# Turning the gathered tokens of experts 2 to 7 by a transposing DMA in place of TensorE transposes

## The chip, the cores and the metric

The kernel runs on one core of one Trainium2 chip. A core has five engines that run on their own and meet by semaphores: TensorE (PE: matrix products from SBUF into PSUM; PEld is its loading of weights), VectorE (DVE), ScalarE (ACT), GpSimd (POOL) and SyncE (SP). Each works through its own queue of instructions in order. DMAs are issued by SP, ACT or POOL. The metric is the device time of one execution in microseconds (us), less is better.

## The reference

Eight batches of pooled attention feed a mixture of eight experts. Every token goes to one expert, and every expert takes `cap` = 4608 / 8 = 576 tokens. Cut to what matters here:

```
x = attention(q, k, v)                 # [4608, 512]
logits = x @ w_gate
# tokens are assigned greedily by falling logit, 576 to an expert
for e in range(8):
    mask = assigned == e
    h = np.maximum(x[mask] @ w1[e], 0.0)   # w1[e]: [512, 1024]
    out[mask] = h @ w2[e]                  # w2[e]: [1024, 512]
```

## The kernel before

Attention comes first (to about 153 us) and writes x to DRAM as `xd`. The experts then run one after the other, in an order that the routing finds while the experts before them run. "Expert 3" below is the fourth in that order.

**Gather.** For one expert `X.gather` (L1035) brings 576 rows of 512 float32 numbers from `xd` into `xg` [128, 5, 512], with one indirect DMA of POOL for each of five token tiles: four of 128 tokens and one of 64. Here a partition holds a token.

**Turn.** A product needs the feature, not the token, along the partitions. So `X.xt(t)` (L1064) turns tile t: four transposes of TensorE (L1073) put it into a PSUM buffer `tp`, ACT copies that to `xh` rounded to the format of fast products (L1075), and DVE puts the rest, what rounding has left over, into `xl` (L1077). `xh` and `xl` [128, 4, 576] have one buffer each.

**Weights.** w1 and w2 of an expert come by SP (L1024, L1032; 2 MB each) into one raw buffer each and are cut in the same way into a high part by ACT (`w1h` L1049, `w2h` L1059) and a low part by DVE (`w1l` L1053, `w2l` L1062), eight pieces each. The load of the next w2 waits until the products of the last token tile (L1136), which read raw w2, are done.

**First stage** (`stage1`, L1079). h = x w1 in two column blocks: tokens 0 to 255 (tiles 0 and 1), then 256 to 575 (tiles 2 to 4), eight groups each. A group is twelve products (L1097) into one of five PSUM buffers `h`; ACT evicts it to `hh` (L1102, in the second block also `hr`, L1104), DVE the rest to `hl` (L1105).

**Second stage** (`stage2`, L1117). For each of four token tiles 24 products (L1131), then ACT copies `yt` out (L1145) and POOL scatters it to the output; the last tile of 64 tokens has 32 products of raw float32 (L1136).

**The order.** Nothing reorders at run time. The function `experts` (L1206) writes all queues out ahead with a planner: `now` counts PE's time as products are issued, `dve` when DVE will be free, and `advance` puts the steps of the routing in where their inputs should be ready. The routing of the next expert is a search on DVE with small products of PE between (`cmp` on DVE L631, then `rt` products L676; `g` on DVE, then `rt` L697; `up` on DVE, and again), four rounds of it, then the numbers of the rows (L785, L804) and the gather. `turns` places a turn once the gather should have landed; tiles 0 to 2 of the next expert go into the second stage of the expert before, tiles 3 and 4 into its own first stage, mostly right behind an `rt` product. The gather of an expert is held back until all five tiles of the expert before are turned.

Of the kernel before, what the change touches and what calls it, by code (L numbers as in the profile page):

```python
# [11 lines left out]
BF = mybir.dt.bfloat16  # L12
F16 = mybir.dt.float16
I32 = mybir.dt.int32
AF = mybir.ActivationFunctionType
OP = mybir.AluOpType
AX = mybir.AxisListType
# [406 lines left out]
class Routing:  # L424
# [28 lines left out]
    def consts(self, jp, ident):  # L453

        nc, cst, J, NC = self.nc, self.cst, self.J, self.NC
        self.ident = ident
        t = self.ti
        self.i36 = cst.tile([128, 36], F32, name="i36")
        nc.vector.tensor_copy(self.i36, t)
        self.tokv = cst.tile([128, NC], F16, name="tokv")  # L460
        nc.vector.tensor_copy(self.tokv, self.tok.rearrange("p b q -> p (b q)"))
        self.j16 = cst.tile([128, J, NC], F16, name="j16")
        nc.scalar.activation(self.j16, self.i36[:, :J, None].to_broadcast([128, J, NC]), AF.Copy)
# [151 lines left out]
    def search(self, shadow, spare):  # L615
# [8 lines left out]
        def compare(*cuts):  # L624
            qb = q16.rearrange("p (b c) -> p b c", c=4)
            for b0, b1 in zip(cuts, cuts[1:]):
                nc.vector.tensor_tensor(cmp[:, b0:b1], qb[:, b0:b1, None].to_broadcast([128, b1 - b0, J, 4]),
                                        self.j16[:, None, :, :4].to_broadcast([128, b1 - b0, J, 4]), op=OP.is_gt)

        def pairs():  # L630
            nc.vector.tensor_tensor(cmp.rearrange("p b j c -> p (b j c)").rearrange("p (c j u) -> p c j u", j=J // 2, u=2),  # L631
# [89 lines left out]
    def close(self, k, last):  # L721
# [46 lines left out]
        def number(b0, b1):  # L768
# [4 lines left out]
        number(*halves[0])  # L773
        OHa = wk.tile([128, 9, 32, 4], F16, name="OHa", bufs=1)
        nc.vector.tensor_tensor(OHa, sf[:, 0].rearrange("p (b q) -> p b q", q=4)[:, :, None].to_broadcast([128, 9, 32, 4]),
                                self.j16[:, None, :, :4].to_broadcast([128, 9, 32, 4]), op=OP.is_equal)
        if not k:
            block(*halves[1])
        yield 2.6, 2.6
# [208 lines left out]
class Experts:  # L988
# [1 line left out]

    def __init__(self, tc, wk, psA, xd, w1, w2, out, ident, cap):
        self.tc, self.nc, self.wk, self.psA = tc, tc.nc, wk, psA
        self.xd, self.w1, self.w2, self.out, self.ident = xd, w1, w2, out, ident
# [64 lines left out]

    def low2(self, e, i):
        self.nc.vector.tensor_tensor(self.w2l[:, i], self.raw2[e][:, i], self.w2h[:, i].bitcast(F32), op=OP.subtract)  # L1062

    def xt(self, t, name="tp", bufs=2, later=lambda after, t, f: f()):  # L1064

# [94 lines left out]
@with_exitstack  # L1160
def kernel(ctx, tc, q, k, v, wblk, moe_w1, moe_w2, out):
    nc = tc.nc
    N, Dm = out.shape
    cap = N // moe_w1.shape[0]
    cst = ctx.enter_context(tc.tile_pool(name="cst", bufs=1))
    dr = ctx.enter_context(tc.tile_pool(name="dr", bufs=1, space=DRAM))
    ctx.enter_context(tc.manual_schedule())
    xd = dr.tile([N, Dm], F32, name="xd")
    lg = cst.tile([128, N // 128, 8], F32, name="lg")
    psR = ctx.enter_context(tc.tile_pool(name="psR", bufs=1, space=PSUM))  # L1170
    A = Attention(tc, cst, psR, q, k, v, wblk, xd, lg)
    rwk = ctx.enter_context(tc.tile_pool(name="rwk", bufs=2))
    R = Routing(tc, cst, rwk, psR, lg, cap)
    A.consts()
    R.first()
    NC = N // 128
    with ExitStack() as c2:
        g = R.run()

        R.poke = lambda numbers: wake(nc, rwk, moe_w2, numbers)  # L1180
        bounds = R.bounds(rwk, NC - 12)
        step = lambda: next(bounds, None)
        start = lambda: next(g)
        A.run(c2, R.ones, lambda: R.consts(A.jp, A.ident), R.more, {NC - 11: [step], NC - 10: [step], NC - 9: [step], NC - 8: [lambda: R.best(0, NC - 8)],
                                                       NC - 7: [start], NC - 6: [start, lambda: wake(nc, rwk, moe_w2, R.ti[:32, 0:1])]},
              R.begin(g), R.warm)
    with ExitStack() as c2:
        rows = cst.tile([128, 6], I32, name="lastrows")

        def keep():  # L1190
            nc.vector.tensor_copy(rows[:, :5], R.rows)
            nc.vector.tensor_copy(rows[:, 5:], R.halves)


        X, flag, ps = experts(c2, tc, g, R, xd, moe_w1, moe_w2, out, A.ident, cap, keep)
        fast, X.scatters, X.fixed = X.scatters, [], True
        with tc.If(flag > 0):  # L1197
# [8 lines left out]
def experts(ctx, tc, g, R, xd, w1, w2, out, ident, cap, keep):  # L1206
# [6 lines left out]
    X = Experts(tc, wk, psB, xd, w1, w2, out, ident, cap)  # L1213

    toks, since, pieces, turned = {}, {}, {}, {}
    held, waiting = [], []

    lows = 0

    fresh, coming, through = False, False, False  # L1220

# [13 lines left out]
    def step(e):  # L1235
# [9 lines left out]
        if what == "id":  # L1245

            if p > e or p and pieces[p - 1].l < 8:
                held.append((p, crit, t, what))
                return False
            X.load_1(R.eid, 0, 4 if p else 2)  # L1250
            eids[p] = R.eid
        elif what == "rows":
            if p and turned[p - 1] < 5:
                held.append((p, crit, t, what))
                return False
            X.gather(R.rows, *R.found)
            if R.found[1] == 5:
                toks[p] = R.rows, R.halves
                turned[p] = 0
# [7 lines left out]
    def advance(e, t, quiet=False):  # L1267

        nonlocal now, fresh
        now += t  # L1270
        fresh = False
        while True:
            if waiting and waiting[0][0] <= now:
                flush(len(waiting) - 1)
            elif ready > now or quiet or first(e) or not step(e):
                break

    def due(e, what, t):
        return (e, what) in since and now >= since[e, what] + t
# [44 lines left out]
    def turn(e, t, name="tp", bufs=2):  # L1324
# [9 lines left out]
        elif (e, t) == (0, 4):  # L1334
            later(1.0, 0.2, lambda: X.load_2(behind(1)))

    def turns(e, upto, late):

        nonlocal last
# [33 lines left out]
    for e in range(8):  # L1373
# [5 lines left out]
        for n, dt in enumerate(X.stage1(later, not e)):  # L1379
# [2 lines left out]
                w1.by(4 + (k + 2) // 8)  # L1382
            if not e and 2 <= n < 96:
                turns(e, 5, 5)
            if n == (84 if e else 40):
                for t in range(turned[e], 5):
                    turn(e, t)
            if n >= 64 and n % 2:
                w2.by((n - 70) // 14 if n > 70 else 0)
            if not more and n == 48:  # L1390
# [5 lines left out]
            elif not more and n == 136:  # L1396
                flag = nc.values_load(flag[0:1, 0:1], min_val=0, max_val=1)
            advance(min(e + 1, 7), dt)
            if e and n < 96:
                turns(e, 5, 3 + (n - 14) // 24)  # L1400
        while w2.l < 8:
            w2.next()
        w1 = pieces[e + 1] = Pieces(e + 1, X.high1, X.low1)
        for n, dt in enumerate(X.stage2(e, *toks[e], range(5 if more else 1))):

            advance(min(e + 1, 7), dt, n >= 96)
            if more and due(e + 1, "id", 9):
                w1.by((n - 60) // 12 if n > 60 else 0)
            if more:
                turns(e + 1, 3, (n - 52) // 12)  # L1410
        if more:
            while e + 1 not in toks:
# [1 line left out]
                step(e + 1)  # L1414
            while w1.l < 4:
                w1.next()
            for t in range(turned[e + 1], 2):
                turn(e + 1, t)
        flush(2)
    flush()  # L1420
    ps = psB.tile([128, 512], F32, name="h", bufs=5)
# [85 lines left out]
```

## Time and profile before

| | |
|---|---|
| time, median of 3 runs | 609.72 us (608.83 to 611.48) |
| the profiled execution's own time | 608.98 us |
| its span in the profile | 607.2 us |
| first and second stage of expert 3 | 28.4 and 27.7 us |
| transposes of gathered tokens, L1073 | 160 (20 for an expert) |

The rows of the profile read as follows. A timeline row has start, busy time, engine, line, operation, output<-inputs, partitions x elements, count, and in brackets the idle time before it with what ended it. Times overlap, since products are pipelined: what an instruction costs its engine is read from the start of it to the start of the next. A row of waits has who waited for whom, total us, times, longest. A row of stages has the stretch, its length, then each engine's busy time.

### The profile page before, as it was taken

How to read it: one execution, taken by the hardware profiler on the slowest of the kernel's cores; microseconds unless marked ns; L12 is line 12 of the kernel's file. 1: busy time of each engine (PE TensorE's matmuls, PEld its weight loads, DVE VectorE, ACT ScalarE, POOL GpSimd, SP SyncE). 2: the span in 40 equal slices, each digit the busy share in tenths (PEclk: the TensorE clock that was granted, in tenths of full speed). 3: DMA queues.
4: the chain of work that ended last, by engine and by line, in shares of the span. 5: the costliest groups of instructions: out<-in, count | busy, mean ns of one | idle time of the engine just before them, and what ended most of it. 6: DMA issues, size and time to landing. Idle time of an engine off the chain costs nothing.

```text
span 607.2 us, 11497 instructions
## 1 busy us (share of the span) xinstructions
PE 588.4 (97%) x4316; PEld 518.5 (85%) x4316; DVE 398.9 (66%) x1187; ACT 239.2 (39%) x562; POOL 177.5 (29%) x222
## 2 busy tenths in 40 slices
PE   8999999985999999999999999999999999999996
PEld 5999999983798799879978987898799889888975
DVE  7678878987896789678972885498278338503400
ACT  7444444461461434333532442254236325513411
POOL 2999999101200500522112301130230123011012
PEclk9999999995999999999999999999999999999999
DMA  8999972223531743418103701640181037014011
GB/s 357 416 425 419 403 284 74 81 98 99 157 125 39 231 166 108 143 40 315 46 36 114 286 1 52 221 161 19 53 320 45 35 135 265 2 52 167 1 40 43
DMA packets 32641, 92.23 MB, mean 152 GB/s; under 512 B 3489, under 2 KB 3489, under 8 KB 29889
## 3 DMA queue, kind: packets, MB, share of 16 engines
q1 hardware_dynamic: 21296, 62.92, 27.6%
q0 software_dynamic: 5952, 19.01, 9.2%
q10 hardware_dynamic: 5328, 9.48, 4.2%
q8 instruction: 35, 0.57, 0.4%
q14 instruction: 30, 0.24, 0.1%
HBM read 72.53 MB, written 18.87 MB: 151 GB/s over the span
## 4 chain that ended last, share of the span: by engine, by line
PE 81%; DVE 8%; issue 7%; ACT 1%; DMA 1%; POOL 1%; POOLq 0%; ACTq 0%; another core or an unknown queue 0%; DVEq 0%
PE h L1097 30%; PE h L1131 25%; PE psa L272 7%; PE pss L227 6%; PE h L1136 4%; PE tp L1073 3%; PE pse L256 2%; PE rt L256 1%; PE rt L676 1%; DVE e L238 1%; PE rt L638 1%; DMA out_dram<-yt,rows 1%; PE rt L217 1%; DMA xg<-xd,rows 1%; PE rt L785 1%
## 5 line engine op out<-in xcount | busy, mean ns | idle before, releaser
L1131 PE MATMUL h<-w2h,hh 128*128 128x512 f32 x256 | 101.5, 396 | 0.3 <-PEq L1197 0.3
L1131 PE MATMUL h<-w2l,hh 128*128 128x512 f32 x256 | 101.0, 395 | 0.0
L1131 PE MATMUL h<-w2h,hl 128*128 128x512 f32 x256 | 100.6, 393 | 0.0
L1111 POOL DMA_INDIRECT out_dram<-yt,rows x29 | 29.4, 1013 | 241.0 <-ACT yt L1145 240.3
L1105 DVE SCALAR_TENSOR_TENSOR hl<-h,hh 128x320 fp32r<-128x320 f32 (+1 forms) x128 | 57.0, 452 | 60.7 <-ACT hh L1102 42.6
L1102 ACT ACTIVATE hh<-h 128x320 fp32r<-128x320 f32 (+1 forms) x128 | 52.6, 411 | 107.3 <-PE h L1097 101.7
L1097 PE MATMUL h<-xh,w1h 128*128 128x320 f32 (+1 forms) x512 | 93.2, 300 | 0.2 <-issue 0.2
L1097 PE MATMUL h<-xl,w1h 128*128 128x320 f32 (+1 forms) x512 | 92.3, 299 | 0.0
L1097 PE MATMUL h<-xh,w1l 128*128 128x320 f32 (+1 forms) x512 | 91.2, 297 | 0.0
L1097 PEld LDWEIGHTS h<-xh,w1h 128*128 128x128 f32 x512 | 75.6, 189 | 3.4 <-issue 3.2
L1097 PEld LDWEIGHTS h<-xl,w1h 128*128 128x128 f32 x512 | 75.9, 189 | 0.4
L1097 PEld LDWEIGHTS h<-xh,w1l 128*128 128x128 f32 x512 | 75.8, 189 | 0.0
L1041 POOL DMA_INDIRECT xg<-xd,rows x40 | 40.9, 1023 | 91.4 <-DVE rows L808 53.1
L1145 ACT ACTIVATE yt<-h 128x512 f32<-128x512 f32 x32 | 19.1, 597 | 109.4 <-PE h L1131 77.8
L272 PE MATMUL psa<-vblk,eT 128*128 128x146 f32 (+3 forms) x390 | 59.9, 302 | 0.2
L1131 PEld LDWEIGHTS h<-w2h,hh 128*128 128x128 f32 x256 | 48.1, 188 | 9.5 <-issue 0.7
L1131 PEld LDWEIGHTS h<-w2l,hh 128*128 128x128 f32 x256 | 48.1, 188 | 9.5
L1131 PEld LDWEIGHTS h<-w2h,hl 128*128 128x128 f32 x256 | 48.1, 188 | 9.0
L272 PEld LDWEIGHTS psa<-vblk,eT 128*128 128x128 f32 (+1 forms) x390 | 50.9, 179 | 1.8 <-POOL kblk L176 0.3
L1077 DVE TENSOR_TENSOR xl<-tp,xh 128x512 fp32r<-128x512 f32 (+1 forms) x40 | 25.3, 632 | 36.5 <-ACT xh L1075 35.2
L1053 DVE TENSOR_TENSOR w1l<-raw,w1h 128x512 fp32r<-128x512 f32 x64 | 41.1, 683 | 8.8 <-ACT w1h L1049 8.6
L1062 DVE TENSOR_TENSOR w2l<-raw,w2h 128x512 fp32r<-128x512 f32 x64 | 43.2, 682 | 3.0 <-ACT w2h L1059 2.8
(225 smaller groups left out, 898.0 us busy)
## 6 DMA issues: line engine op xcount, KB each, us to landing
raw<-in_moe_w_dram SPq DMA_DIRECT2D x64, 512.0 KB, 5.3
xd<-xt ACTq DMA_DIRECT2D x36, 256.0 KB, 6.5
rawv<-in_v_dram SPq DMA_DIRECT2D x7, 1280.0 KB, 14.1
rawk<-in_k_dram SPq DMA_DIRECT2D x7, 1152.0 KB, 13.2
rawq<-in_q_dram SPq DMA_DIRECT2D x7, 1152.0 KB, 10.4
rawk<-in_k_dram SPq DMA_DIRECT2D x2, 576.0 KB
rawv<-in_v_dram SPq DMA_DIRECT2D x1, 768.0 KB
rawq<-in_q_dram SPq DMA_DIRECT2D x1, 640.0 KB, 9.0
```

The lines of the kernel that those rows point to most:

```text
L227: nc.tensor.matmul(ps[cols, j // 2, 144 * (j % 2):144 * (j % 2) + 144], self.q_of(b, j, n, cols.stop - cols.start), self.kblk[b % 4][:, j] ...
L272: self.nc.tensor.matmul(o[h], self.eT[i][:, c, h], self.vblk[b % 4][:, self.BLOCKS[c]:self.BLOCKS[c + 1]], start=(c == cs[0]), stop=(c == ...
L1041: nc.gpsimd.indirect_dma_start(out=self.xg[:n, t, :], out_offset=None, in_=self.xd, in_offset=bass.IndirectOffsetOnAxis(ap=rows[:n, t:t + ...
L1053: self.nc.vector.tensor_tensor(l, raw, h.bitcast(F32), op=OP.subtract)
L1062: self.nc.vector.tensor_tensor(self.w2l[:, i], self.raw2[e][:, i], self.w2h[:, i].bitcast(F32), op=OP.subtract)
L1077: later(1.3, 0.65, lambda: nc.vector.tensor_tensor(xl, ps[:, :, :n], xh, op=OP.subtract))
L1097: nc.tensor.matmul(ps[:, :m], a[:, j, fs], b[:, j, o], start=(n == 0), stop=(n == 11))
L1102: nc.scalar.activation(hh[:, f, o], ps[:, :m], AF.Relu)
L1105: later(0.65, 0.4, lambda f=f, o=o, m=m, ps=ps: nc.vector.scalar_tensor_tensor(hl[:, f, o], ps[:, :m], 0.0, hh[:, f, o].bitcast(F32), op0= ...
L1111: st = nc.gpsimd.indirect_dma_start(out=rows, out_offset=bass.IndirectOffsetOnAxis(ap=idx, axis=0), in_=y, in_offset=None)
L1131: nc.tensor.matmul(ps, a[:, f, o], b[:, f], start=(f == 0 and k == 0), stop=(f == 7 and k == 2))
L1136: nc.tensor.matmul(ps[64 * a:64 * a + 64, :256], self.hr[:, f], self.raw2[e][:, f, 256 * a:256 * a + 256], start=(f == 0), stop=(f == 7))
```

## The change

For experts 2 to 7 the five turns by TensorE go, and each tile takes this way instead:

1. `split(t)`: ACT reads the gathered tile as 16-bit numbers and writes two planes, the low halves and the high halves of all 512 features, into `planes` [128, 2, 512]; ACT then issues a DMA that stores them in DRAM (`xs`).
2. `swap(t)`: SP issues a transposing DMA, which reads the 256 rows of 512 16-bit numbers of a tile from `xs` and writes them turned into the place in `xg` from which the tile came. Since low and high halves of a token are neighbouring rows, they end as neighbours, and the result read as float32 is the turned tile.
3. `high(t)`: ACT rounds it into `xh`, from SBUF now; `low(t)`: DVE puts the rest into `xl`.

The planner orders the four steps: `swap` 4.4 us of its clock after the split, `high` 8.6 after it, `low` 0.8 after `high`. Splits are at least 2.3 apart. `hurry` lets a step that writes `xh` or `xl` pass only when the first stage of the expert before is behind it (`xfree`). The splits of experts 3 to 7 may thus begin in the first stage of the expert before, those of expert 2 in the second stage of expert 1. The gather of each of the experts 3 to 7 is held until `low` has run for all five tiles of the expert before. `j16`, a table of constants, shrinks from 36 columns to 4. Experts 0 and 1 keep their TensorE turns.

```diff
+    def split(self, t):
+        nc = self.nc
+        n = min(128, self.cap - 128 * t)
+        p = self.wk.tile([128, 2, 512], U16, name="planes", bufs=2)
+        nc.scalar.activation(p[:n], self.xg[:n, t].bitcast(U16).rearrange("p (d h) -> p h d", h=2), AF.Copy)
+        nc.scalar.dma_start(self.xs[t, :n], p[:n])
+
+    def swap(self, t):
+        n = min(128, self.cap - 128 * t)
+        self.nc.sync.dma_start_transpose(self.turned(t).bitcast(U16), self.xs[t, :n].rearrange("p h d -> (p h) d"))
+
+    def turned(self, t):
+        n = min(128, self.cap - 128 * t)
+        return self.xg[:, t, :4 * n].rearrange("p (j m) -> p j m", j=4)
+
+    def high(self, t):
...
+        self.nc.scalar.activation(self.xh[:, :, o], self.turned(t), AF.Copy)
+
+    def low(self, t):
+        o = slice(128 * t, min(128 * t + 128, self.cap))
+        self.nc.vector.tensor_tensor(self.xl[:, :, o], self.turned(t), self.xh[:, :, o].bitcast(F32), op=OP.subtract)
...
-            if p and turned[p - 1] < 5:
+            if p and (done.get(p - 1, 0) if p > 2 else turned[p - 1]) < 5:
...
+        while (k := hurry()) is not None and soon[k][0] <= now:
+            soon.pop(k)[2]()
...
+    def swap(e, t):
+        def high():
+            X.high(t)
+            soon.append((now + 0.8, e, low))
+        def low():
+            nonlocal dve
+            X.low(t)
+            dve = max(dve, now) + 0.65
+            done[e] = t + 1
+        X.split(t)
+        turned[e] = t + 1
+        soon.extend(((now + 4.4, 0, lambda: X.swap(t)), (now + 8.6, e, high)))
+
+    def swaps(e):
+        nonlocal last
+        t = turned.get(e, 5)
+        if t < 5 and due(e, "rows", 7.0 + 1.3 * t) and now >= last + 2.3:
+            last = now
+            swap(e, t)
+
+    def hurry():
+        soon.sort(key=lambda x: x[0])
+        for k, (d, e, f) in enumerate(soon):
+            if e <= xfree:
+                return k
+        return None
...
-            if e and n < 96:
+            if e == 1 and n < 96:
                 turns(e, 5, 3 + (n - 14) // 24)
+            if e > 1 and n < 90:
+                swaps(e)
+            elif e > 1 and more and n > 100:
+                swaps(e + 1)
...
+        xfree = e + 1
...
-            if more:
+            if e and more:
+                swaps(e + 1)
+            elif more:
                 turns(e + 1, 3, (n - 52) // 12)
```

**ACT, from the end of expert 3's first stage into its second.** `hh` and `hr` are evictions of the first stage, `yt` of the second, `w1h` pieces of the next expert's weights. Before:

```order
L1059 ACTIVATE w2h<-raw_4470 128x512
L1102 ACTIVATE hh<-h 128x320
L1104 ACTIVATE hr<-h 128x64
L1102 ACTIVATE hh<-h 128x320
L1104 ACTIVATE hr<-h 128x64
L1049 ACTIVATE w1h<-raw_4489 128x512 x5
L1145 ACTIVATE yt<-h 128x512
L1075 ACTIVATE xh<-tp 128x4x128 x3
L1145 ACTIVATE yt<-h 128x512
L1049 ACTIVATE w1h<-raw_4489 128x512 x3
```

And now:

```order
L1060 ACTIVATE w2h<-raw_4475 128x512
L1070 ACTIVATE planes<-xg 64x1024
L1071 DMA xs<-planes 64x1024
L1132 ACTIVATE hh<-h 128x320
L1134 ACTIVATE hr<-h 128x64
L1132 ACTIVATE hh<-h 128x320
L1134 ACTIVATE hr<-h 128x64
L1088 ACTIVATE xh<-xg 128x4x128 x4
L1050 ACTIVATE w1h<-raw_4494 128x512 x2
L1175 ACTIVATE yt<-h 128x512
L1088 ACTIVATE xh<-xg 128x4x64
L1050 ACTIVATE w1h<-raw_4494 128x512 x3
```

The split and the store of the fifth tile stand two evictions ahead of the stage's end (the other four further up, between evictions), and all five `xh` stand early in the second stage, where there were three, later, and two in the first stage behind.

**DVE, at the same place.** `hl` is the last rest of the first stage; `up`, `q` and `cmp` are the search of the routing, which PE's next `rt` product (L676, now L677) reads. Before:

```order
L1062 TENSOR_TENSOR w2l<-raw_4470,w2h 128x512
L1105 SCALAR_TENSOR_TENSOR hl<-h,hh 128x320
L1053 TENSOR_TENSOR w1l<-raw_4489,w1h 128x512 x4
L699 TENSOR_REDUCE up<-rt 128x1
L587 TENSOR_SCALAR q_4957<-q32c,up 128x72
L631 TENSOR_TENSOR cmp<-q_4957,jv 128x1152
```

And now:

```order
L1063 TENSOR_TENSOR w2l<-raw_4475,w2h 128x512
L1135 SCALAR_TENSOR_TENSOR hl<-h,hh 128x320
L1092 TENSOR_TENSOR xl<-xg,xh 128x4x128 x4
L1054 TENSOR_TENSOR w1l<-raw_4494,w1h 128x512 x2
L1092 TENSOR_TENSOR xl<-xg,xh 128x4x64
L1054 TENSOR_TENSOR w1l<-raw_4494,w1h 128x512 x2
L700 TENSOR_REDUCE up<-rt 128x1
L588 TENSOR_SCALAR q_4994<-q32c,up 128x72
L632 TENSOR_TENSOR cmp<-q_4994,jv 128x1152
```

All five `xl` now stand ahead of the search. On PE the product that reads this `cmp` stood behind 30 products of the second stage and stands behind 45 now.

**SP, between the loads of expert 3's w1 and w2.** Now:

```order
L1025 DMA raw_3825<-in_moe_w_dram 128x2x512
L1076 DMA_TRANSPOSE xg<-xs 128x4x256 x4
L1076 DMA_TRANSPOSE xg<-xs 128x4x128
L1029 TENSOR_LOAD eid
L1029 ISA x2
L1033 ISA
L1033 DMA raw_4475<-in_moe_w_dram 128x2x512
```

The five transposing DMAs stand behind the load of an expert's w1 and ahead of that of its w2; the loads are in the order that they had.

More of the change, by code (lines that the diff above doesn't have):

```diff
@@ L14 @@
 I32 = mybir.dt.int32
+U16 = mybir.dt.uint16
 AF = mybir.ActivationFunctionType
@@ L461, in consts @@
         nc.vector.tensor_copy(self.tokv, self.tok.rearrange("p b q -> p (b q)"))
-        self.j16 = cst.tile([128, J, NC], F16, name="j16")
-        nc.scalar.activation(self.j16, self.i36[:, :J, None].to_broadcast([128, J, NC]), AF.Copy)
+        self.j16 = cst.tile([128, J, 4], F16, name="j16")
+        nc.scalar.activation(self.j16, self.i36[:, :J, None].to_broadcast([128, J, 4]), AF.Copy)
         self.jv = cst.tile([128, J], F16, name="jv")
@@ L627, in compare @@
                 nc.vector.tensor_tensor(cmp[:, b0:b1], qb[:, b0:b1, None].to_broadcast([128, b1 - b0, J, 4]),
-                                        self.j16[:, None, :, :4].to_broadcast([128, b1 - b0, J, 4]), op=OP.is_gt)
+                                        self.j16[:, None].to_broadcast([128, b1 - b0, J, 4]), op=OP.is_gt)
         def pairs():
@@ L775, in close @@
         nc.vector.tensor_tensor(OHa, sf[:, 0].rearrange("p (b q) -> p b q", q=4)[:, :, None].to_broadcast([128, 9, 32, 4]),
-                                self.j16[:, None, :, :4].to_broadcast([128, 9, 32, 4]), op=OP.is_equal)
+                                self.j16[:, None].to_broadcast([128, 9, 32, 4]), op=OP.is_equal)
         if not k:
@@ L988, with __init__ @@
 class Experts:
-    def __init__(self, tc, wk, psA, xd, w1, w2, out, ident, cap):
+    def __init__(self, tc, wk, psA, xd, xs, w1, w2, out, ident, cap):
         self.tc, self.nc, self.wk, self.psA = tc, tc.nc, wk, psA
-        self.xd, self.w1, self.w2, self.out, self.ident = xd, w1, w2, out, ident
+        self.xd, self.xs, self.w1, self.w2, self.out, self.ident = xd, xs, w1, w2, out, ident
         self.cap = cap
@@ L1062, in low2 @@
         self.nc.vector.tensor_tensor(self.w2l[:, i], self.raw2[e][:, i], self.w2h[:, i].bitcast(F32), op=OP.subtract)
+    def split(self, t):
[11 more added lines that the diff above has]
+    def high(self, t):
+        if t == 0:
+            self.xh = self.buf("xh", [128, 4, 576], F32R)
+            self.xl = self.buf("xl", [128, 4, 576], F32R)
+        o = slice(128 * t, min(128 * t + 128, self.cap))
+        self.nc.scalar.activation(self.xh[:, :, o], self.turned(t), AF.Copy)
+    def low(self, t):
+        o = slice(128 * t, min(128 * t + 128, self.cap))
+        self.nc.vector.tensor_tensor(self.xl[:, :, o], self.turned(t), self.xh[:, :, o].bitcast(F32), op=OP.subtract)
     def xt(self, t, name="tp", bufs=2, later=lambda after, t, f: f()):
@@ L1168 @@
     xd = dr.tile([N, Dm], F32, name="xd")
+    xs = dr.tile([5, 128, 2, Dm], U16, name="xs")
     lg = cst.tile([128, N // 128, 8], F32, name="lg")
@@ L1192, in keep @@
             nc.vector.tensor_copy(rows[:, 5:], R.halves)
-        X, flag, ps = experts(c2, tc, g, R, xd, moe_w1, moe_w2, out, A.ident, cap, keep)
+        X, flag, ps = experts(c2, tc, g, R, xd, xs, moe_w1, moe_w2, out, A.ident, cap, keep)
         fast, X.scatters, X.fixed = X.scatters, [], True
@@ L1203, with experts @@
             pass
-def experts(ctx, tc, g, R, xd, w1, w2, out, ident, cap, keep):
+def experts(ctx, tc, g, R, xd, xs, w1, w2, out, ident, cap, keep):
     nc = tc.nc
@@ L1212, in experts @@
     psB = ctx.enter_context(tc.tile_pool(name="psB", bufs=1, space=PSUM))
-    X = Experts(tc, wk, psB, xd, w1, w2, out, ident, cap)
+    X = Experts(tc, wk, psB, xd, xs, w1, w2, out, ident, cap)
     toks, since, pieces, turned = {}, {}, {}, {}
-    held, waiting = [], []
+    held, waiting, soon, done = [], [], [], {}
     lows = 0
+    xfree = 0
     fresh, coming, through = False, False, False
@@ L1335, in turn, with swapped @@
             later(1.0, 0.2, lambda: X.load_2(behind(1)))
+    def swap(e, t):
[4 more added lines that the diff above has]
+        def low():
+            nonlocal dve
+            X.low(t)
[16 more added lines that the diff above has]
+        return None
+    def swapped(e, upto):
+        nonlocal now, last
+        for t in range(turned[e], upto):
+            now = last = max(now, last + 2.3)
+            swap(e, t)
+        while done.get(e, 0) < upto:
+            d, _, f = soon.pop(hurry())
+            now = max(now, d)
+            f()
     def turns(e, upto, late):
@@ L1384, in experts @@
                 turns(e, 5, 5)
-            if n == (84 if e else 40):
+            if n == (84 if e else 40) and e < 2:
                 for t in range(turned[e], 5):
                     turn(e, t)
+            if n == 95 and e > 1:
+                swapped(e, 5)
             if n >= 64 and n % 2:
@@ L1416, in experts @@
                 w1.next()
-            for t in range(turned[e + 1], 2):
-                turn(e + 1, t)
+            if e:
+                swapped(e + 1, 2)
+            else:
+                for t in range(turned[e + 1], 2):
+                    turn(e + 1, t)
         flush(2)
```

## The prediction

> **What bounds the kernel now.** I read the page first, then the waits of the engine that it names, then the stages one by one.
>
> ```profile
> span 607.2 us, 11497 instructions
> PE 588.4 (97%) x4316; PEld 518.5 (85%) x4316; DVE 398.9 (66%) x1187; ACT 239.2 (39%) x562; POOL 177.5 (29%) x222
> ```
>
> TensorE (PE) is busy for 97% of the span. A busy PE need not be the bound of every stage, so the second view is PE's waits from 271 us to the end, where experts 2 to 7 run:
>
> ```profile
> PE h L1131 <- PEq L1197: 0.3, 1, 0.3
> PE rt L676 <- DVE cmp L631: 0.3, 1, 0.3
> ```
>
> Two waits, 0.6 us in 336 us. In these stages nothing but PE's own queue sets the end, and a PE microsecond taken away comes off the end unless something new is late. The third view is the busy time by stage (stretch; its length, then PE, PEld, DVE, ACT, POOL, the clock, the DMA share, GB/s): second stage of expert 1, first stage of expert 2, then both stages of expert 3.
>
> ```profile
> 242.60:271.40 28.80, 28.64 (x180) 21.58 (x179) 21.00 (x70) 8.90 (x17) 10.38 (x14) 1.00 0.30 99
> 271.40:300.10 28.70, 28.45 (x242) 27.75 (x241) 24.52 (x85) 12.34 (x33) 6.29 (x7) 1.00 0.57 193
> 328.30:356.70 28.40, 28.40 (x242) 27.79 (x241) 23.44 (x76) 12.12 (x33) 5.89 (x7) 1.00 0.55 195
> 356.70:384.40 27.70, 27.70 (x162) 21.21 (x160) 13.90 (x44) 8.80 (x17) 4.51 (x8) 1.00 0.10 39
> ```
>
> ACT has 16 us to spare in a stage and more in a second stage; DVE has 4 to 5 us in a first stage. DMA is nearly idle in a second stage. The clock column is 1.00 throughout.
>
> **What goes.** Six experts lose five turns of four transposes each. What one costs PE is read from where its neighbours start:
>
> ```profile
> 366.07 0.18 PE L697 MATMUL rt<-g,ones 128*128 128x8 bf16 x1
> 366.11 0.63 PE L1073 MATMUL tp<-ident,xg 128*128 128x128 f32 x4
> 366.50 0.48 PE L1131 MATMUL h<-w2h,hh 128*128 128x512 f32 x1
> 366.81 0.40 PE L1131 MATMUL h<-w2h,hl 128*128 128x512 f32 x1
> ...
> 390.34 0.51 PE L785 MATMUL rt<-OHb,OHa 128*128 128x80 f16 x9
> 390.78 0.46 PE L1073 MATMUL tp<-ident,xg 64*128 64x64 f32 x4
> 391.17 0.74 PE L1097 MATMUL h<-xl,w1h 128*128 128x256 f32 x4
> ...
> 482.47 0.39 PE L1131 MATMUL h<-w2h,hl 128*128 128x512 f32 x1
> 482.70 0.60 PE L1073 MATMUL tp<-ident,xg 128*128 128x128 f32 x4
> 483.05 0.48 PE L1131 MATMUL h<-w2l,hh 128*128 128x512 f32 x1
> 483.37 0.39 PE L1131 MATMUL h<-w2h,hh 128*128 128x512 f32 x1
> ```
>
> From 366.11 to 366.50 a turn takes 0.39 us; the half-size one takes the same (390.78 to 391.17). The product behind it needs 0.31 instead of 0.23 us, but that step is paid behind the routing matmul anyway, which stays. Where a turn stands between two products, as at 482.70, both go: 0.35 + 0.32 - 0.23 = 0.44. Of the 30 turns 22 follow a routing matmul and 8 (three of expert 6, five of expert 7) stand alone: 22 x 0.39 + 8 x 0.44 = **12.1 us** off PE. With the step counted for all it would be 30 x 0.47 = 14.1; that is the upper end.
>
> **What comes, on ACT.** Thirty splits of 1,024 halves, and each issues a store:
>
> ```profile
> 6.63 1.15 ACT L463 ACTIVATE j<-i 128x1152 f16<-128x1152 f32 x1
> 8.95 0.46 ACT L149 ACTIVATE kblk<-psa 64x72 f32<-64x72 f32 x2 [1.18 <-PE psa L146]
> 9.44 0.74 ACT L497 ACTIVATE blk<-i 128x648 bf16<-128x648 f32 x1
> ...
> L302 ACTq DMA_DIRECT2D xd<-xt x36: 326/326/353, 22.1 to 137.3; - x36
> ...
> 346.86 0.44 ACT L1102 ACTIVATE hh<-h 128x320 fp32r<-128x320 f32 x1
> 347.18 0.23 ACT L1104 ACTIVATE hr<-h 128x64 f32<-128x64 f32 x1
> 347.28 0.65 ACT L1059 ACTIVATE w2h<-raw 128x512 fp32r<-128x512 f32 x1
> 347.80 0.46 ACT L1102 ACTIVATE hh<-h 128x320 fp32r<-128x320 f32 x1
> ...
> 349.69 0.75 PE L1097 MATMUL h<-xh,w1l 128*128 128x320 f32 x4
> 350.27 0.75 PE L1097 MATMUL h<-xl,w1h 128*128 128x320 f32 x4
> ```
>
> Between 648 and 1,152 elements ACT takes 0.41 us more, 0.81 ns each, so a split is 0.74 + 376 x 0.81 ns = 1.05 us; with the store's issue 1.4. For experts 3 to 7 they stand in the second half of the first stage of the expert before. There PE takes 0.58 us for four products (349.69 to 350.27), 1.76 for the 12 of a group, 14.1 for the eight groups; ACT has eight evictions (hh and hr, 0.42 from 346.86 to 347.28), six w2h (0.52 to 347.80) and five splits: 3.4 + 3.1 + 7.0 = 13.5. It just fits, and ACT will run 1 to 2 us behind PE at the end. That costs PE nothing: five h buffers let evictions lag by four groups, 7 us. The smaller j16 saves 0.9 us of ACT at 6.6 us, where ACT then idled 1.18 us: no gain.
>
> **What comes, on the queues.** The store has a row, the turning transfer has none:
>
> ```profile
> xd<-xt ACTq DMA_DIRECT2D x4, 256.0 KB, 2.0
> DMA to landing us min/median/max: 2.0/6.5/10.1
> DMA packets 463, 1.54 MB, mean 38 GB/s; under 512 B 96, under 2 KB 96, under 8 KB 459
> SPq L1032 <- PE h L1136: 189.5, 7, 34.1
> ```
>
> The same 256 KB landed in 2.0 us at 128 to 140 us, where the queues were quiet, and took up to 10.1 under loads. From 400 to 440 us, when the splits of expert 5 will run, DMA carries 38 GB/s, so a store is 2.0. For the turned read I bound it by those ends, 2.0 and 10.1, and take **4.0**: the same bytes on quiet queues, and as much again for writing them in 16-bit pieces. On SP only w2's load stands behind the transfers, and it waits for L1136 at the end of the second stage anyway.
>
> **Who waits for it.** The fifth tile is the critical one. Its split ends about 0.5 us into the second stage (ACT is late), its store lands at 2.5. Behind its xl on DVE the new order has two w1l and then the search of the routing, whose matmul PE meets after 45 products:
>
> ```profile
> 337.03 0.41 DVE L1077 TENSOR_TENSOR xl<-tp,xh 128x256 fp32r<-128x256 f32 x1
> ...
> 357.89 2.50 DVE L1053 TENSOR_TENSOR w1l<-raw,w1h 128x512 fp32r<-128x512 f32 x4
> 362.28 0.17 DVE L699 TENSOR_REDUCE up<-rt 128x1 f32<-128x8 f32 x1 [1.90 <-PE rt L697]
> 362.49 0.26 DVE L587 TENSOR_SCALAR q<-q32c,up 128x72 f16<-128x72 f32 x1
> 362.78 0.76 DVE L631 TENSOR_TENSOR cmp<-q,jv 128x1152 bf16<-128x1152 f16 x1
> ```
>
> 45 x 0.23 = 10.4 us. Back from there: 1.3 for up, q and cmp, 1.25 for two w1l, 0.41 for xl, about 0.5 for xh and the handing over: the tile must be there at 6.9, which leaves the turned read 6.9 - 2.5 = **4.4 us**. Four fit, with little over. For expert 2 the splits lie in expert 1's second stage and the room is about as small, so I charge 0.6 us of new waits in all. xl itself reads SBUF in place of PSUM: w1l does that now, 2.50 / 4 = 0.63 us for 512 elements, no dearer.
>
> The sum: profiled execution 608.98 - 12.1 + 0.6 = **597.5 us**. That execution lies 0.7 below the median shown, 609.72, against which faster and slower are counted; 0.5% of it, about what a measurement can tell, is 3.0 us.
>
> On the unknown price the pages disagree. The Trainium skill (VectorE: DVE Perf Modes, The three transpose paths) gives 1,309 ns for a 128x128 block of 16-bit numbers by DMA; eight blocks are a tile, an estimate of 10.5 us if they run one behind the other, and the change would lose. The Trainium skill (DMA: Bandwidth & Descriptors, Latency and other measured facts) gives 261 GB/s for turning transfers, an estimate of 1.0 us for 256 KB, and the sum would stand. No run here shows either yet.
>
> **The rivals.**
>
> - *The turned tile is a little late.* If it lands in 5.4 us, each of six experts waits 1.0 us: 597.5 + 6 = 603.5. For it: ACT's tightness in the stretch. Against: a second stage has idle queues.
> - *The transfer is slow: slower than before.* One mechanism: the turned read, then xh on ACT, xl on DVE, the search behind it, and PE in its queue at the matmul after product 45. It decides from 4.4 + 12.1 / 6 = 6.4 us. At 10.1, the far end, six experts lose 5.7 each: 597.5 + 34 = 631.5; if tiles also go one behind the other, more. Against: the 10.1 was seen under the attention part's loads, not on quiet queues. The block price of the Trainium skill's first page above would be this case.
> - *The freed time is not the bound.* If PE were held by DVE's search and only met it earlier, most of the 12.1 would come back as waits: 607. The first stage of expert 2, where DVE is busy 24.5 of 28.7 us and PE waited 0.3 for cmp, speaks for a part of it; the other stages, without a wait, against.
>
> **How the numbers follow.** Forecast 0.60 (595 to 601); a little late 0.17 (601 to 607, nearly all of it faster by over 0.5%); slow transfer 0.17; freed time not the bound 0.06. Faster 0.74, within 0.5% 0.09, slower 0.17. The range goes from 595, where the steps behind the turns go too, to 609, and leaves out the slow transfer alone.
>
> **What will show it.** No transposes into tp after those of expert 1, and stages of experts 3 to 6 shorter by 0.39 x 5 = 2 us: the first term. ACT groups of planes at 1.05 us and stores landing in 2: the second. Landing of the xg transfers at or under 4.4 us and no PE wait for cmp longer than a few tenths: the third. If PE waits at the routing matmuls of second stages, with DVE at xl before them, the little-late or the slow rival holds, and the landing says which. A landing over 6.4 us would make the prediction wrong.

## The result, and the profile after

The changed kernel took 601.49 us (median of 4 runs, 600.75 to 603.39), the kernel before 609.74 us (608.83 to 611.48): a ratio of 0.987, 95% interval 0.983 to 0.990. It is faster by 1.35%. The profiled execution took 601.85 us.

The page's span and first part, of the changed kernel:

```profile
span 600.1 us, 11440 instructions
PE 578.1 (96%) x4196; PEld 508.7 (85%) x4196; DVE 400.4 (67%) x1187; ACT 265.7 (44%) x592; POOL 180.5 (30%) x222
```

PE is busy 10.3 us less and the span is 7.1 us shorter: some of what PE no longer does came back as idle time. The waits of PE from 240 us to the end say where:

```profile
PE rt L677 <- DVE cmp L632: 2.3, 3, 1.1
PE rt L698 <- DVE g L692: 1.8, 2, 1.0
PE h L1161 <- PEq L1228: 0.3, 1, 0.3
```

4.1 us at the matmuls of the routing's search, where the kernel before had 0.4 from there on. Nowhere does PE wait for `xh` or `xl` themselves. By stage (the stretches are those of before: second stage of expert 1, first of 2, both of 3; then both of expert 5):

```profile
244.50:272.00 27.50, 27.48 (x169) 20.48 (x167) 19.37 (x68) 12.69 (x20) 10.24 (x14) 1.00 0.68 186
272.00:299.40 27.40, 27.40 (x234) 27.00 (x233) 24.89 (x82) 15.73 (x37) 5.81 (x7) 1.00 0.72 230
327.70:356.90 29.20, 27.78 (x234) 26.89 (x233) 21.95 (x71) 15.52 (x34) 5.80 (x7) 1.00 0.74 249
356.90:383.50 26.60, 26.60 (x151) 20.15 (x149) 15.97 (x49) 9.95 (x21) 4.56 (x8) 1.00 0.22 64
439.30:465.80 26.50, 26.50 (x214) 26.37 (x213) 20.05 (x67) 13.17 (x31) 5.80 (x7) 1.00 0.74 252
465.80:491.30 25.50, 25.50 (x130) 20.08 (x128) 9.71 (x18) 12.16 (x25) 4.71 (x8) 1.00 0.33 90
```

The first column behind the stretch is its length, the next PE's busy time. Most stages got shorter by 0.9 to 1.7 us, but the first stage of expert 3 got longer, 28.4 to 29.2, with 1.4 us in which PE did nothing. Expert 4's first stage is as long (29.2), and the second of expert 2 has a wait of 1.1 us. Experts 5 and 6, in whose stages no search of the routing stands, got the whole gain: 54.4 to 52.0 and 54.6 to 52.0 us for both stages.

Expert 3's first stage shows how. ACT first, then DVE, then PE (start, busy time, ..., idle before it and what ended it):

```profile
342.98 0.38 ACT L1132 ACTIVATE hh<-h 128x256 fp32r<-128x256 f32 x1 [2.63 <-PE h L1127]
344.95 1.06 ACT L1070 ACTIVATE planes<-xg 128x1024 uint16<-128x1024 uint16 x1
346.04 0.34 ACTq L1071 DMA_DIRECT2D xs<-planes  x1
346.42 0.63 ACT L1060 ACTIVATE w2h<-raw 128x512 fp32r<-128x512 f32 x1 [0.41 <-ACT planes L1070]
...
349.39 0.42 ACT L1132 ACTIVATE hh<-h 128x320 fp32r<-128x320 f32 x1
349.71 0.22 ACT L1134 ACTIVATE hr<-h 128x64 f32<-128x64 f32 x1
```

```profile
349.96 0.49 DVE L1135 SCALAR_TENSOR_TENSOR hl<-h,hh 128x320 fp32r<-128x320 f32 x1 [1.34 <-ACT hr L1134]
350.37 0.68 DVE L1063 TENSOR_TENSOR w2l<-raw,w2h 128x512 fp32r<-128x512 f32 x1
350.97 0.14 DVE L683 TENSOR_TENSOR lack<-need,rt 32x8 f32<-32x8 f32 x1
...
351.53 0.17 DVE L692 TENSOR_TENSOR g<-rt,lack 32x8 bf16<-32x8 f32 x1
```

```profile
340.17 0.75 PE L1127 MATMUL h<-xh,w1h 128*128 128x320 f32 x4
...
351.75 0.18 PE L698 MATMUL rt<-g,ones 128*128 128x8 bf16 x1 [0.84 <-DVE g L692]
355.10 0.39 PE L677 MATMUL rt<-oh,cmp 128*128 128x32 bf16 x9 [0.57 <-DVE cmp L632]
```

The product that the eviction at 342.98 reads had ended when PE began the next, at 340.17; what held ACT until 342.98 the trace does not show. ACT begins the second half of the stage late, cannot catch up among the splits, and evicts late. DVE stands at `hl`, released by ACT's `hr`; the search's `lack` and `g` are behind it in DVE's queue, and PE, also in order, stands at the search's matmul. In expert 2's second stage, with its 1.1 us, DVE stood 1.99 us for an `w1h` that came behind the last split in ACT's queue. A split holds ACT 1.47 us (344.95 to 346.42), the store's issue and 0.41 us of idle time with it.

Expert 5's first stage had the same idle time on ACT, but no search behind it, and took 26.55 us, as it did without that idle time in the later traces:

```profile
454.57 0.38 ACT L1132 ACTIVATE hh<-h 128x256 fp32r<-128x256 f32 x1 [2.63 <-PE h L1127]
```

From this come two theories. **A:** ACT, filled by the splits, has no reserve in these halves; its lag reaches PE through DVE's queue and the search. **B:** the turned reads land too late, or the search is late for a reason of its own.

### The profile page after: what moved, and what is told of

The parts are those of the page before. It is cut to its first block, busy times and chain, and to the rows that moved or that the text cites. A ratio compares the mean times of both kernels' runs of the same rounds, so it can differ in the third digit from the quotient of the medians.

```text
span 600.1 us, 11440 instructions
## 1 busy us (share of the span) xinstructions
PE 578.1 (96%) x4196; PEld 508.7 (85%) x4196; DVE 400.4 (67%) x1187; ACT 265.7 (44%) x592; POOL 180.5 (30%) x222
## 2 busy tenths in 40 slices
DMA packets 65184, 106.38 MB, mean 177 GB/s; under 512 B 32576, under 2 KB 32576, under 8 KB 62432
## 4 chain that ended last, share of the span: by engine, by line
PE 69%; issue 14%; DVE 7%; ACT 4%; POOL 3%; DMA 2%; POOLq 1%; ACTq 1%; another core or an unknown queue 0%; DVEq 0%
PE h L1127 24%; PE h L1161 21%; PE psa L273 7%; PE pss L228 6%; PE h L1166 4%; PE pse L257 2%; POOL out_dram L1141 2%; ACT planes L1070 1%; PE rt L257 1%; PE tp L1103 1%; POOL xg L1042 1%; PE rt L677 1%; DVE e L239 1%; PE rt L639 1%; PE rt L218 1%
## 5 line engine op out<-in xcount | busy, mean ns | idle before, releaser
L1141 POOL DMA_INDIRECT out_dram<-yt,rows x29 | 33.2, 1143 | 232.1 <-ACT yt L1175 231.2
L228 PE MATMUL pss<-kblk,rawq 128*128 128x144 f32 (+1 forms) x320 | 43.8, 294 | 0.3 <-DVE e L239 0.3
```

The source lines that it names most:

```text
L228: nc.tensor.matmul(ps[cols, j // 2, 144 * (j % 2):144 * (j % 2) + 144], self.q_of(b, j, n, cols.stop - cols.start), self.kblk[b % 4][:, j] ...
L1141: st = nc.gpsimd.indirect_dma_start(out=rows, out_offset=bass.IndirectOffsetOnAxis(ap=idx, axis=0), in_=y, in_offset=None)
```

## The experiments

Each run stands beside runs of the kernel before on the same chip; ratios are to those.

**1. The changed kernel again.** No edit.

> The changed kernel once more, nothing altered. Ratio to before 0.983 to 0.990. What is asked of its trace: in the first comparison the changed kernel reached the second stage of expert 1 some 1.95 us later than before, ahead of any changed instruction on TensorE. If that is a difference between one execution and the next, this trace starts that stage within 0.5 us of 242.6 us or at a third value; if the change brings it (the smaller table j16, or memory laid out otherwise), it stands at 244.5 again. The waits of TensorE for the routing's search (lines 698 and 677) in the first stages of experts 3 and 4 should come back at about 3 us in all under either theory.

596.51 us (5 runs, 596.07 to 599.89), ratio 0.981 (0.979 to 0.983), with one wait of 0.4 us at L698. The second stage of expert 1 began at 243.2, not 244.5. The expected 3 us of waits did not come back: the same kernel is 5.0 us faster here, and the kernel before is not (609.21). By the traces 3.7 us of this are waits at the search and 1.3 us the earlier start of that stage.

**2. Stores issued by SP.**

```diff
-        nc.scalar.dma_start(self.xs[t, :n], p[:n])
+        nc.sync.dma_start(self.xs[t, :n], p[:n])
```

> The store of the planes is issued by SyncE instead of ScalarE; nothing else. Theory A (ScalarE is too full in the second half of the first stages of experts 3 and 4; its evictions come late, VectorE stalls at hl, the search of the routing behind it on VectorE comes late, and TensorE waits for the search): a split then costs ScalarE about 1.06 us and not 1.47, three or four splits stand in such a half, so 1.2 to 1.6 us of lag go; TensorE's waits at lines 698 and 677 in these stages fall from 2.95 us to under 1.5, and the time falls by 1 to 2 us against the changed kernel, to a ratio to before of about 0.983 to 0.985. Theory B (the late search comes from VectorE's own added work, or from the routing's own chain, not from ScalarE): these waits stay at about 3 us and the ratio stays at 0.9866 within 0.002. If SyncE's queue matters (a store holds the transposing reads and weight loads behind it), turned tiles land later, the waits of xh for them grow past 7.0 us, and the time rises.

595.70 us, ratio 0.978 (0.977 to 0.980): 0.8 below the changed kernel on the same chip, though the two intervals overlap, so that the time alone does not show a gain. No wait of PE at the search is left. The direction is A's; the size is small since only 0.4 us of waits were there to win.

**3. No early splits.**

```diff
-            elif e > 1 and more and n > 100:
-                swaps(e + 1)
```

> No split stands in the first stage of the expert before any more; the splits of an expert begin with the second stage of the expert before. Theory A: ScalarE has its old load in the second halves of the first stages of experts 2 to 4, TensorE's 2.95 us of waits at lines 698 and 677 in the first stages of experts 3 and 4 go, and if the later splits fit, the time falls by 2 to 3 us against the changed kernel, to a ratio of about 0.982. What stands against it: the splits and the turned reads then crowd the second stages and the first halves, and where a turned tile is late TensorE waits at the first matmul that reads it; then the ratio is 0.987 or more, with waits of TensorE for xh or xl. Theory B: the waits for the search stay as they are.

597.33 us, ratio 0.981 (0.979 to 0.983), no better than the changed kernel. With the waits of A nearly absent on this chip it had nothing to win and tells nothing on A. Waits of `xh` for `xg` on ACT grew to 14.5 us, and PE did not pay for them (0.9 us of waits at the search).

**4. Split and store by POOL.**

```diff
-        nc.scalar.activation(p[:n], self.xg[:n, t].bitcast(U16)..., AF.Copy)
-        nc.scalar.dma_start(self.xs[t, :n], p[:n])
+        nc.gpsimd.tensor_copy(p[:n], self.xg[:n, t].bitcast(U16)...)
+        nc.gpsimd.dma_start(self.xs[t, :n], p[:n])
```

> GpSimd copies the planes and issues their store; ScalarE has neither. Theory A: all of the 1.47 us per split leaves ScalarE, the waits for the search in the first stages of experts 3 and 4 (2.95 us) go, and the time falls by about 3 us against the changed kernel: ratio about 0.981 to 0.983. What stands against it is GpSimd's own price, which no trace here shows: a copy of 128x1024 16-bit elements there may take from 1 to some 5 us, and its in-order queue holds the scatters and the gather; if it takes over about 4 us the turned tiles come late (waits of xh for xg and of TensorE for xh), and the ratio is above 0.99. Theory B: waits for the search stay.

604.66 us, ratio 0.994 (0.992 to 0.997), 8 us worse than the changed kernel and a miss. The trace is of its fastest run, 602.36. POOL's copy costs 1.05 us, as on ACT. The price is DVE's, in the timeline at 293 us:

```profile
293.59 2.17 DVE L1063 TENSOR_TENSOR w2l<-raw,w2h 128x512 fp32r<-128x512 f32 x1
294.15 1.05 POOL L1070 COPY planes<-xg 128x1024 uint16<-128x1024 uint16 x1
```

A `w2l` of 0.68 us takes 2.17 while POOL copies; DVE's busy time rose from 399.8 (run 1) to 417.4 us, and PE waited 6.1 us at L677. ACT was as free as A asks, but the search was late by DVE's own slowness: the way from DVE to PE is the same.

**5 to 8. Why run 1 differs from the first comparison.** The row at 342.98 above has 2.63 us of idle time put down to a product. The second trace has nothing there. So: the kernel before once more for its trace, the changed kernel a third time, and both with a stall added:

```diff
+            if n == 95 and 2 <= e < 7:
+                for _ in range(4):
+                    nc.scalar.activation(X.w2h[:, 5], X.raw2[e][:, 5], AF.Copy)
```

> The kernel before once more, for its trace beside the changed kernel's on one chip. In the first pair of traces ScalarE began the eviction of the last product of a first half (line 1102, 128x256) up to about 1 us after w2h's copies ended and the product had ended, with no releaser that fits; in the changed kernel's first trace the same place had 2.63 us (342.98 us), and in its second trace nothing (338.25 us). If that idle time belongs to the chip or the run and not to the change, this trace shows it at the same places whenever the changed kernel's next trace does, and neither shows it otherwise.

> The changed kernel a third time, as a control for the two kernels with added ScalarE work. Either the first result comes back (about 0.987, with the 2.6 us stalls of ScalarE before the last eviction of a first half and about 4 us of waits of TensorE at lines 677 and 698), or the second (about 0.981, without both). A result with the stalls and without the waits, or the other way round, speaks against the theory that the stalls make the waits.

> Changed kernel with four extra ScalarE copies (128x512, about 0.57 us each, 2.3 us) put just ahead of the last eviction of the first half of the first stages of experts 2 to 6. The copies write a piece of w2h that is written again later, so nothing else changes. Theory A (ScalarE, filled by the splits, cannot make up a delay of 2 to 3 us in the second half; VectorE stalls at hl and the search of the routing behind it makes TensorE wait): waits at lines 698 and 677 appear in the first stages of experts 3 and 4, 1 to 1.7 us each, and in the second stage of expert 2; nothing in experts 5 and 6, where no search stands in that half. Time 2 to 4.5 us above the changed kernel of the same call. Rival (the 5 us between the two results of the changed kernel come from the clock or the early part alone, and the lag is harmless): time within 0.7 us of the changed kernel.

> Kernel before with the same four extra ScalarE copies at the same places. Theory A: without splits ScalarE has 5 us or more to spare in the second half and makes the 2.3 us up, so the ratio to before is 1.000 within 0.0015. Rival (any delay of ScalarE of this size at this place costs TensorE time, splits or not): 2 us or more slower, ratio 1.003 to 1.008.

The kernel before took 608.87 us and the changed one 596.77, ratio 0.980 (0.979 to 0.982): 12.1 us between them. ACT at the same eviction, in the first trace of before, in the new trace of before, in the third of the changed kernel and in the padded changed kernel:

```profile
342.93 0.39 ACT L1102 ACTIVATE hh<-h 128x256 fp32r<-128x256 f32 x1 [1.02 <-PE h L1097]
343.21 0.62 ACT L1059 ACTIVATE w2h<-raw 128x512 fp32r<-128x512 f32 x1
345.90 0.44 ACT L1102 ACTIVATE hh<-h 128x320 fp32r<-128x320 f32 x1 [2.07 <-PE h L1097]
```

```profile
341.81 0.38 ACT L1102 ACTIVATE hh<-h 128x256 fp32r<-128x256 f32 x1
342.09 0.62 ACT L1059 ACTIVATE w2h<-raw 128x512 fp32r<-128x512 f32 x1
343.57 0.44 ACT L1102 ACTIVATE hh<-h 128x320 fp32r<-128x320 f32 x1 [0.86 <-PE h L1097]
```

```profile
338.03 0.38 ACT L1132 ACTIVATE hh<-h 128x256 fp32r<-128x256 f32 x1
```

```profile
338.12 2.62 ACT L1474 ACTIVATE w2h<-raw 128x512 fp32r<-128x512 f32 x4
340.64 0.37 ACT L1132 ACTIVATE hh<-h 128x256 fp32r<-128x256 f32 x1
```

In the first comparison both kernels had the stall: before, the eviction of 343.57 came at 345.90, 2.3 us late. In the later traces neither has it. So the stall is not of the change. What it costs is: the padded kernel before took 609.12 us (ratio 1.001, 1.000 to 1.002), so a stall of 2.5 us in five stages costs it nothing; the padded changed kernel took 598.74 (0.983, 0.981 to 0.984), 2.0 us more than unpadded. Its waits of PE from 240 us, the unpadded one's ahead of them:

```profile
PE rt L677 <- DVE cmp L632: 0.8, 2, 0.6
PE rt L698 <- DVE g L694: 0.4, 1, 0.4
PE h L1161 <- PEq L1228: 0.3, 1, 0.3
```

```profile
PE rt L677 <- DVE cmp L632: 2.2, 4, 0.6
PE h L1161 <- PEq L1228: 0.3, 1, 0.3
```

Theory A is shown by this pair: the same delay is free without splits and is paid with them, at the search. The first stages of experts 3 and 4 took 28.2 us each with the pad and 27.5 and 27.6 without; of the padded kernel before they took 28.2, as unpadded. The size was under the expectation: 0.6 us of wait in each of these two stages, not 1 to 1.7, and none in the second stage of expert 2. The pad costs less than the first comparison lost, and leaves ACT less behind: there a second stall of 0.64 us followed.

The unpadded trace holds something of theory B too. Of its 0.8 us at L677, 0.6 lie in the second stage of expert 4, and there a turned tile came late (ACT, DVE and PE in the third trace of the changed kernel):

```profile
412.75 0.63 ACT L1088 ACTIVATE xh<-xg 128x512 fp32r<-128x512 f32 x1 [2.64 <-DMA xg<-xs]
413.42 0.69 DVE L1092 TENSOR_TENSOR xl<-xg,xh 128x512 fp32r<-128x512 f32 x1 [2.00 <-ACT xh L1088]
418.29 0.39 PE L677 MATMUL rt<-oh,cmp 128*128 128x32 bf16 x9 [0.63 <-DVE cmp L632]
```

**9. Pad and SP's stores together.** Edits 2 and 5 to 8.

> The stores are issued by SyncE, as in the kernel that moved them, and the four extra ScalarE copies of the padded changed kernel (2.5 us) stand before the last eviction of the first half of the first stages of experts 2 to 6. Theory A: with 0.4 to 0.5 us less per split on ScalarE, three or four splits per half, the delay left for the search is 1.5 to 2 us smaller, so the pad costs under 1 us against the kernel with SyncE's stores alone (ratio 0.978 to 0.981), where it cost the changed kernel 2.0 us. Rival (the pad costs TensorE a fixed time whatever else ScalarE does, 2 us as before): ratio about 0.982 with waits at line 677 of 2 us.

596.23 us, ratio 0.979 (0.977 to 0.980), against 0.978 without the pad: the pad's 2.0 us are gone, and the first stages of experts 3 and 4 took 27.3 us each, as without it. About 0.4 us off each split decide whether this stall is paid.

**10. Every turned read twice.**

```diff
+        for _ in range(2):
-        self.nc.sync.dma_start_transpose(self.turned(t)..., self.xs[t, :n]...)
+            self.nc.sync.dma_start_transpose(self.turned(t)..., self.xs[t, :n]...)
```

> Changed kernel with every turned read issued twice into the same place, so that the tile is ready only when the second has landed: from a median of 3.6 us (2.4 to 5.6 in the second trace of the changed kernel) to about 7 us. Theory B (the room behind a split is some 4 to 6 us, and a turned read beyond it is paid by TensorE): waits of xh for xg on ScalarE grow from 4.8 us to 15 us or more, VectorE's xl come late, and TensorE waits in the second stages or at the start of the next first stage, 1 us or more for each of six experts: ratio 0.988 to 1.0. Theory A alone (only what fills ScalarE in the first stages matters, the transfer has room to spare): waits of xh grow, but the ratio stays under 0.984.

646.52 us, ratio 1.061 (1.058 to 1.064): far more than B expected. SP's row says why the size is no measure of lateness alone:

```profile
306.94 24.61 SPq L1077 DMA_TRANSPOSE xg<-xs  x10
```

The second read of a tile waits for the first in SP's queue, so five tiles go one behind the other, 4.9 us each. PE waited 31.8 us at L677 and 8.5 at L698, in the first stage of expert 2 and the second stages of experts 2 to 4, which took 38 to 40 us each. Experts 5 and 6 kept their 26.6 and 25.5 us: without a search behind it, even a read twice as long costs nothing. The waits, 40.3 us, are not the whole price of 50: the granted clock was 0.56 in the 4 us behind one wait of 8.51 us.

**11. Expert 1 too.** A set `S = (1, ..., 7)` takes the place of the tests `e > 1`, with SP's stores.

> Expert 1 takes the transposing DMA too (experts 1 to 7), and the stores are issued by SyncE. If the term of the prediction carries over (five turns of 0.39 to 0.44 us on TensorE removed for one more expert, nothing new waited for), about 2 us below the kernel with SyncE's stores alone: ratio 0.974 to 0.976. What stands against it: the second stage of expert 0 and the first of expert 1 hold the longest search of the routing and the first full loads of weights, so turned tiles or the search come late and TensorE waits there; ratio 0.978 or more, with waits before 275 us that the kernel with SyncE's stores has not.

607.27 us, ratio 0.996 (0.994 to 0.998): 11.6 us above run 2 in place of 2 below it. What the expectation set against the gain came true. PE at the start of expert 1's first stage, and ACT ahead of it:

```profile
219.31 0.58 PE L1127 MATMUL h<-xh,w1h 128*128 128x256 f32 x1 [6.38 <-ACT xh L1088]
```

```profile
206.41 1.06 ACT L1070 ACTIVATE planes<-xg 128x1024 uint16<-128x1024 uint16 x1 [0.80 <-DMA xg<-xd,rows]
...
215.54 0.63 ACT L1088 ACTIVATE xh<-xg 128x512 fp32r<-128x512 f32 x1 [0.72 <-DMA xg<-xs]
```

The gather lands only 206 us into the run, and from split to `xh` a tile takes 9.1 us. Here the stage that needs it begins before the tile is through, and PE pays without any search between; two more waits, 1.3 us for `xh` and 1.9 for `xl`, follow in the same stage.

**12. One more landing, without the row on SP.** POOL's queue copies each stored tile in DRAM, and the turned read reads the copy.

```diff
+        nc.gpsimd.dma_start(self.xs2[t, :n], self.xs[t, :n])
```

> Changed kernel with one more step in DRAM: GpSimd's queue copies each stored tile of planes to a second place, and the turned read reads that. SyncE still issues one read per tile, so the reads do not stand in a row behind one another as in the kernel that issued each twice, where five tiles took 24.6 us of SyncE's queue; a tile only comes later, by one more landing of 2 to 3 us (store: median 2.8 us). Theory B by the prediction's working (4.4 us of room for a read of 4.0 us taken and 3.6 us measured, TensorE pays from 6.4 us on): 2 to 3 us more lies at that edge, so TensorE waits at line 677 in second stages by some tenths to 1 us per expert, and the ratio is 0.982 to 0.988. If there is no room left at all, as the kernel with the doubled reads could also be read, each expert pays 2 to 3 us or more: ratio 0.995 to 1.01. If there is more room than worked out: ratio 0.979 to 0.982 and waits of xh for xg only somewhat above 4.8 us.

622.25 us, ratio 1.020 (1.018 to 1.022): worse than any of the three expectations. DVE and PE in the second stage of expert 2:

```profile
310.68 0.69 DVE L1093 TENSOR_TENSOR xl<-xg,xh 128x512 fp32r<-128x512 f32 x1 [3.27 <-ACT xh L1089]
...
317.88 0.76 DVE L632 TENSOR_TENSOR cmp<-q,jv 128x1152 bf16<-128x1152 f16 x1
318.70 0.42 PE L677 MATMUL rt<-oh,cmp 128*128 128x32 bf16 x9 [4.63 <-DVE cmp L632]
```

The `xl` of late tiles stand in DVE's queue ahead of the search. PE waited 19.9 us at the search in all. POOL's scatters wait too, behind copies that wait for a store (89.6 us in all), which this edit adds besides; how much of the 26 us is theirs is not separated. Experts 5 and 6 again kept 26.6 and 25.5 us.

## Why the prediction was right, step by step

- **The sum.** 597.5 against 601.49 in the first comparison: inside the range, but 0.5 us outside the forecast band of 595 to 601 and in that of the little-late rival. In the two repeats 596.51 and 596.77. That these come within 1 us of the sum is in part luck, since both terms were too small and the errors cancel.
- **The turns, 12.1 us.** Too small. The 12.1 us between the two medians of runs 5 to 8 are the gain less what the waits that are left cost. In run 2, where PE waits for no search, the medians differ by 609.21 - 595.70 = 13.5 us, and from the second stage of expert 1 to the end its trace is 13.9 us shorter than the new trace of before (run 2 first):

```profile
244.41:594.80 350.39, 345.48 (x2320) 300.55 (x2318) 204.77 (x614) 156.61 (x337) 77.28 (x100) 1.00 0.49 153
242.79:607.10 364.31, 359.10 (x2440) 312.26 (x2438) 203.68 (x614) 130.47 (x307) 68.70 (x100) 1.00 0.31 108
```

  That is 0.46 us for a turn, close to the 0.47 from which the prediction made its upper end of 14.1, and not 0.39. Experts 5 and 6, without waits, gained 2.3 and 2.6 us, where five turns were counted as 2.0 to 2.2.
- **The split, 1.05 us.** Measured 1.06. With its store 1.47, not 1.4: ACT stood idle 0.41 us between a split and its next activation, with 0.34 of it the issue.
- **"That costs PE nothing: five h buffers let evictions lag."** This step failed. The buffers do hold the products, but PE is reached another way: ACT late, DVE at `hl`, the search behind `hl`, PE at the search's matmul. With 1.47 per split ACT had 3.4 + 3.1 + 5 x 1.47 = 13.85 of 14.1 us to do in the half, so a stall of 2.6 us was paid, where one of 2.5 us was free in the kernel before. The term for new waits, 0.6 us, was 4.1 in the first comparison and 0.4 and 1.2 in the repeats; by the length of the same stretch, 351.5 and 352.3 us against run 2's 350.4, the repeats lost 1.1 and 1.9.
- **The places.** The prediction looked for waits in second stages. One of 1.1 us was there, in expert 2; three us lay in the first stages of experts 3 and 4, which it had put at nothing.
- **The turned read, 4.0 us; the store, 2.0.** The sum of both, 6.0, was nearly right: the medians add to 6.4. The landings of the store and of the turned read in run 1 (min/median/max):

```profile
DMA to landing us min/median/max: 2.0/2.8/4.7
DMA to landing us min/median/max: 2.4/3.6/5.6
```

  Neither estimate is near what was measured. Eight blocks at the 1,309 ns of the Trainium skill (VectorE: DVE Perf Modes, The three transpose paths) made an estimate of 10.5 us for a tile if they run one behind the other; the slowest landing is 5.6. The 261 GB/s of the Trainium skill (DMA: Bandwidth & Descriptors, Latency and other measured facts) made an estimate of 1.0 us; the quickest landing is 2.4. No run here gives the time of one block alone or the rate of such reads in a stream.
- **The room, 4.4 us, and the slow rival from 6.4 on.** The mechanism is shown by runs 10 and 12, and once, with 0.6 us, in the third trace of the changed kernel itself: late tiles, `xl` ahead of the search, PE at L677. The price was too small: in run 12 tiles later by one more landing, and POOL's waits with them, cost about 26 us and not some tenths per expert; a waiting `xh` also stands ahead of the next split in ACT's queue. And it is not six experts that pay: the price lies in the stages up to expert 4's, which have a search.
- **The freed time not the bound.** Refuted by run 2: no wait at the search is left there, and the time is 13.5 us shorter. Experts 5 and 6, without a search, say nothing on it.
- **A little late, 603.5.** Near the first comparison's time, in the main by another cause: there ACT was late, not the tiles.

The 1.95 us by which the first trace of the changed kernel lay behind ahead of any changed instruction on PE shrank to 0.6 and 0.4 us against the first trace of before in the repeats; it belongs to the execution. From 155 to 160 us the granted clock was 0.51 in the first trace of the changed kernel, 1.00 in the first of before and 0.99 in the third of the changed kernel, and the first stage of expert 0 took 29.4 us and not 28.3; why the clock differed is open. The smaller j16 was not tried alone.

Of the versions run, the one with SP's stores has the lowest median, 595.70 us, ratio 0.978; its lead on the changed kernel is within the noise.

## What to carry to other kernels

Work moved off the bounding engine to one with time to spare is free only as long as that engine keeps a reserve in each half of a stage: 13.85 of 14.1 us is none, and the first stall is passed on. When you ask who waits for a late engine, follow every in-order queue behind it, not the buffers alone: here the lag went from ACT through DVE to a small matmul of another task in PE's queue. A way through DRAM of 9 us is hidden where the data are gathered a whole stage ahead, and is paid in full where they are not.

## What the hardware showed that was not expected

- ACT stood idle for up to 2.75 us ahead of evictions at the middle of the first stages of experts 3 to 5 in both kernels of the first comparison, with a product as the named releaser that had ended long before; the three later traces of these kernels lack it. What held ACT is open, and no run here was made on it; the pad only imitates it.
- A copy by POOL tripled a DVE operation beside it (2.17 us for 0.68). The Trainium skill (Advanced Engine Details and Errata, VectorE Performance Modes) says that VectorE's second SBUF port is shared with GpSimd and that GpSimd's instructions and VectorE's two-port ones interfere with or block each other. Run 4 shows DVE slowed beside POOL, though not whether `w2l` is such an instruction, and it puts the loss at 17.6 us of DVE's time for 33.1 us of POOL's copies.
- The new transfers took the packets under 512 B from 3,489 to 32,576 and the DMA share of expert 3's first stage from 0.55 to 0.74.
- Behind long waits of PE the granted clock was lower in runs 10 and 12. In run 12, behind the 4.63 us of 318.70, it was 0.50, and products that step 0.23 us apart elsewhere in that stage stood 0.43 apart:

```profile
318.70:322.70 4.00, 4.00 (x19) 2.90 (x19) 2.33 (x10) 1.42 (x3) 0.00 (x0) 0.50 0.31 98
```
